# A two-layer attention kernel on one core: the first two query chunks walked side by side, group by group

## The chip, the core and the metric

The kernel runs on one core of a Trainium2 chip. TensorE (PE in the profile) multiplies, ScalarE (ACT) takes the exponentials, VectorE (DVE) copies and divides, SyncE (SP) issues most of the DMAs. The metric is device time in microseconds (us), the median over runs of the whole program.

## The reference, cut to what matters

Four blocks on one x of 2048 rows by 1024 columns, with 32 heads of 32 columns: A, B, A, B, each `x = x + block(layernorm(x))`. A is linear attention. B is softmax attention, and only B is touched by the change:

```python
def _B_ref(x, wqkv, wo):
    qkv = (x @ wqkv).reshape(B, S, 3, H, Dh).transpose(2, 0, 3, 1, 4)
    q, k, v = qkv[0], qkv[1], qkv[2]
    scores = einsum("bhqd,bhkd->bhqk", q, k) * (Dh ** -0.5)
    p = softmax(scores, axis=-1)
    o = einsum("bhqk,bhkd->bhqd", p, v)
    return o.transpose(0, 2, 1, 3).reshape(B, S, D) @ wo
```

## The kernel before

The program first records every operation with its engine, an estimated duration, its dependences, its buffers and a priority number. Then `Sched.run` plays the operations through once, engine by engine, lowest priority number first, nothing further than `WINDOW` = 40 ahead of the lowest number not yet begun, and no class of buffers over its `QUOTA`. The order that comes out is the order in which each engine's instructions are written. On the chip an engine does not leave that order.

There are two layers, each an A block and then a B block. The B block of a layer is `attention` (base number `at`). The 2048 queries are four chunks of 512 (`qc` 0 to 3), the 32 heads are eight groups of four (`g` 0 to 7). In this text a **unit** is one query chunk with one group. A unit has 64 score blocks (two head pairs `pp`, eight `d`, four `j`), each 128 keys by 512 queries. Three blocks make one **exp**: three score matmuls (line 827) into three PSUM banks, one ACT activation over 128x1536 (line 833), and then the matmuls of line 862, which multiply the exponentials by the values and by ones and add up in bank 6. The scores have banks 0 to 2 and 3 to 5 in turn, so PE can be at most two exps ahead of ACT. A unit has 21⅓ exps, a B block 32 units and 683 exps. At a unit's end DVE copies the accumulator (line 874), two DMAs move the sums (lines 881 and 883), DVE takes reciprocals (line 885) and multiplies (line 889); the result is an `oT` tile.

Everything else that PE does in the meantime goes through the one bank that is left, bank 7 (`FIL`). This text calls it **filler**: eight matmuls of 128x512 (line 586, in four **pieces** of two), and a DVE instruction that empties the bank. There are four kinds:

- `b_k(g, c, ...)`: keys of group g from chunk c of the input, 28 for groups 1 to 7; emptied by line 741, then four DMAs (line 733).
- `b_v(1, c, t, ...)`: values for groups 4 to 7, 16 of them.
- `b_q(g, qc, ...)`: queries of one unit, 31; emptied by line 749, then two DMAs (lines 751 and 752).
- `b_o` (layer 0) and `b_last` (layer 1, line 788): the output projection of a query chunk, once all eight of its `oT` tiles are there, 8 for a chunk. After chunk 3 they are not filler: they stand behind the attention, in any bank.

Before the change the units go chunk by chunk: (0,0), (0,1) ... (0,7), (1,0) ... (3,7). So all keys and values must be there by the end of the first eight units, and the numbers put `b_k` of group g at `at + 10*(g-1) + 1 + c`. Weights come as 256 KB loads (`w2`, line 446) or as 1 MB loads (`slab`).

Of the kernel before, what the change touches and what calls it, by code (L numbers as in the profile page):

```python
# [9 lines left out]
ACT = mybir.ActivationFunctionType  # L10
# [8 lines left out]
C512 = 512  # L19
# [26 lines left out]
class Sched:  # L46
# [87 lines left out]
    def run(self):  # L134
# [23 lines left out]
        while left:  # L158
# [56 lines left out]
WIDE = 3  # L215
WINDOW = 40.0
QUOTA = {"pk": 3, "pv": 2, "kv": 1, "ln": 2, "mm": 2, "cmp": 2, "bc": 2, "num": 1, "wt": 4, "fil": 2,
         "e": 6, "vp": 6, "E": 5, "q2": 3, "kt": 3, "w2": 8, "oT": 13, "T": 4, "den": 4, "lnt": 6, "lnw": 2,
         "eq": 8, "ns": 4, "cw": 6, "hl": 6, "oc": 2, "slab": 7, "fin": 4, "rs": 8}


# [8 lines left out]
MM = 0.2165  # L230
# [3 lines left out]
def kernel(  # L234
# [22 lines left out]
    B_w = B_wqkv.rearrange("(po pi) f -> pi po f", pi=P)  # L257
# [66 lines left out]
    op = sch.op  # L324
# [57 lines left out]
    xdone = [None] * NC  # L382
# [381 lines left out]
    def b_o(ft, c, prio, w, oT, banks):  # L764
        wb, ww, wd = w
        pb, pv = ps("fil", banks)
        m = mmg2(pb, pv, lambda po: ww()[:, po, :], lambda po: oT[po][1](),
                 [[oT[2 * i][2], oT[2 * i + 1][2]] for i in range(4)], wd,
                 [wb] + [oT[i][0] for i in range(G)], prio)
# [3 lines left out]
    def b_last(c, t, fc, prio, w, oT, banks, eng):  # L773

        wb, ww, wd = w
        pb, pv = ps("fil", banks)
        ts = slice(t * P, (t + 1) * P)
        xs = slice(c * C512 + t * P, c * C512 + (t + 1) * P)

        def resid():  # L780
            for k in range(4):
                nc.tensor.matmul(pv()[:, k * P:(k + 1) * P], lhsT=xT[:, 4 * fc + k, xs], rhs=ident[:],
                                 start=False, stop=(k == 3), skip_group_check=True)
        m = None
        for i in range(4):
# [4 lines left out]
            m = op("PE", 2 * MM, fn, flat([m, oT[2 * i][2], oT[2 * i + 1][2], wd[i]]),  # L790
                   [pb, wb, oT[2 * i][0], oT[2 * i + 1][0]], prio, mode="n")
        m = op("PE", 0.4, resid, [m], [pb], prio, mode="n")
        r_b, r_v = sb("fin", C512)
        e = evac(eng, r_v, pv, m, [pb, r_b], prio)
        dma(prio, lambda: nc.sync.dma_start(
            out=out[0, xs, fc * C512:(fc + 1) * C512], in_=r_v()), [e], [r_b], kb=128)

    def attention(base, kT, vT, q_of, gate):
# [10 lines left out]
        while i < len(units):  # L809
# [3 lines left out]
            s_b, s_v = ps("S", [tuple(range(lo, lo + w))])  # L813
            e_b, e_v = sb("E", WIDE * C512)
            qc, g, pp, d, j = grp[0]
            prio = base + 100 * qc + 10 * g + 5 * pp + 0.5 * d
            deps, bufs = [], []
            for u in grp:
                deps += flat([kT[u[1]][2][u[3] // 2], q_of[(u[0], u[1])][2]])
# [17 lines left out]
                e_of[u] = (e_b, e_v, x)  # L837
            i += w
            n += 1
        oTs = {}  # L840
        for qc in range(NC):
            oTs[qc] = {}
            for g in range(G):
                T = []
                for pp in range(2):
                    a_b, a_v = ps("acc", [(6,)])
                    last = None
                    for d in range(8):
                        prio = base + 100 * qc + 10 * g + 5 * pp + 0.5 * d
# [27 lines left out]
                prio = base + 100 * qc + 10 * g + 12  # L877
# [16 lines left out]
        return oTs  # L894


    xnA, xnB = {}, {}
    load_x()
    phi_ld = [dma(0.0, lambda j=j: nc.scalar.dma_start(
# [3 lines left out]
    for layer in range(2):  # L903
# [57 lines left out]
        for qc in range(NC):  # L961
            for g in range(G):
                if qc or g:
                    w = slab("w2", at + 100 * qc + 10 * g - 9, B_w[:, :, g * P:(g + 1) * P], P)
                    q_of[(qc, g)] = b_q(g, qc, at + 100 * qc + 10 * g - 6, w, FIL)
        oTs = attention(at, kT, vT, q_of, gate)
        last = layer == 1
        if last:
            bo_s = [slab("slab", at + 100 + fc, B_o[:, :, fc * C512:(fc + 1) * C512], C512) for fc in range(2)]
        for qc in range(NC):  # L970
            end = qc == NC - 1
            pr = at + 100 * (qc + 1)
            banks = ANY if end else FIL
            if last:
                for t in range(TB):
                    for fc in range(2):
                        b_last(qc, t, fc, pr + 20 + 8 * (2 * t + fc), bo_s[fc], oTs[qc], banks,
                               ("ACT", "DVE")[fc] if end else "DVE")
# [39 lines left out]
```

## Time and profile before

| | |
|---|---|
| median of 3 runs | 2840.84 us (2840.16 to 2841.62) |
| the profiled execution, its own time | 2833.51 us |
| its span, first to last instruction | 2831.7 us |
| PE, ACT, DVE busy over the span | 89%, 78%, 38% |
| first to last exp of layer 0 | 422.9 to 1406.3 us |
| first to last exp of layer 1 | 1815.1 to 2804.3 us |

The profiled execution is 7.3 us faster than the median; sums below are made against it. Busy shares are means over very unlike stages, and a busy PE need not be the bound: its matmuls are recorded with their latencies, and take longer when its clock is lower.

### The profile page before, as it was taken

The numbers are of one execution on the slowest core, as the hardware profiler recorded it, in microseconds if no ns is written. First come the engines' busy times: TensorE is split into PE (matmuls) and PEld (weight loads), VectorE is DVE, ScalarE is ACT, GpSimd is POOL, SyncE is SP. The second block draws the span as 40 slices with busy tenths as digits, with TensorE's granted clock in tenths as the row PEclk, the third lists the DMA queues.
The fourth block names the chain that finished last, engine by engine and source line by source line (L and its number), as shares of the span: only waits on it lengthen the run. The fifth ranks groups of instructions, "written<-read, shape, count | busy, mean of one in ns | idle before, by whom it ended". The sixth has DMA issues, their size and how long they took to land.

```text
span 2831.7 us, 42740 instructions
## 1 busy us (share of the span) xinstructions
PE 2520.0 (89%) x17984; PEld 804.2 (28%) x17984; DVE 1071.1 (38%) x1435; ACT 2211.7 (78%) x1931; POOL 22.4 (1%) x70
## 2 busy tenths in 40 slices
PE   6989989998898888888899999899988888888887
PEld 3543332222222222222144333222222222222222
DVE  4966652333222232222278666333322222222222
ACT  5325447789999999999842445477999999999996
POOL 0000000000000000000000000000000000000000
PEclk9999999999888888888699999899988978988987
DMA  8100003112201210210040000211211011011100
GB/s 179 53 31 3 5 9 75 36 35 47 45 19 29 46 26 21 47 33 14 22 123 8 31 5 2 54 38 32 68 40 27 25 27 29 23 27 36 25 16 23
DMA packets 213120, 101.40 MB, mean 36 GB/s; under 512 B 152512, under 2 KB 203712, under 8 KB 212928
## 3 DMA queue, kind: packets, MB, share of 16 engines
q1 hardware_dynamic: 208704, 94.42, 14.0%
q10 hardware_dynamic: 4224, 4.26, 0.6%
q8 instruction: 140, 2.29, 0.4%
q14 instruction: 52, 0.43, 0.1%
HBM read 50.40 MB, written 8.39 MB: 21 GB/s over the span
## 4 chain that ended last, share of the span: by engine, by line
PE 43%; ACT 39%; issue 10%; DVE 5%; DMA 2%; SPq 1%; ACTq 0%; DVEq 0%; POOL 0%; POOLq 0%
ACT arena L833 37%; PE psum L586 23%; PE psum L862 8%; PE psum L827 6%; SPq L389 1%; PE psum L788 1%; PE psum L677 1%; PE psum L562 1%; DVE arena L438 1%; DVE arena L434 1%; PE psum L368 1%; DMA arena<-arena 1%; ACT arena L404 1%; PE psum L664 1%; PE psum L701 0%
## 5 line engine op out<-in xcount | busy, mean ns | idle before, releaser
L833 ACT ACTIVATE arena<-psum 128x1536 bf16<-128x1536 f32 (+1 forms) x1366 | 1857.7, 1506 | 114.9 <-PE psum L827 86.7
L586 PE MATMUL psum<-arena 128*128 128x512 bf16 x3840 | 1029.3, 389 | 43.8 <-DVE arena L438 18.4
L862 PE MATMUL psum<-arena 128*32 128x512 bf16 x4096 | 856.7, 441 | 24.3 <-ACT arena L833 16.0
L862 PE MATMUL psum<-arena,ones_bf 128*32 128x512 bf16 x4096 | 856.9, 441 | 0.0
L827 PE MATMUL psum<-arena 32*128 32x512 bf16 x4096 | 600.8, 430 | 188.6 <-ACT arena L833 177.1
L586 PEld LDWEIGHTS <-arena 128*128 128x128 bf16 x3840 | 312.2, 98 | 510.2 <-issue 258.1
L827 PEld LDWEIGHTS <-arena 32*128 32x128 bf16 x4096 | 180.9, 92 | 712.4 <-issue 702.7
L862 PEld LDWEIGHTS <-arena 128*32 128x32 bf16 x4096 | 176.1, 96 | 514.2 <-issue 512.4
L874 DVE COPY arena<-psum 128x512 f32<-128x512 f32 x128 | 88.5, 691 | 555.1 <-PE psum L862 555.1
L885 DVE RECIPROCAL arena<-arena 128x128 f32<-128x128 f32 x256 | 217.7, 910 | 109.5 <-DMA arena<-arena 98.8
L749 DVE TENSOR_SCALAR arena<-psum 128x512 bf16<-128x512 f32 x64 | 44.2, 691 | 492.2 <-PE psum L827 353.8
L531 ACT ACTIVATE arena<-psum 128x512 bf16<-128x512 f32 x128 | 69.8, 603 | 163.9 <-PE psum L586 101.7
L862 PEld LDWEIGHTS <-ones_bf 128*32 128x32 bf16 x4096 | 177.9, 96 | 59.4 <-issue 57.5
L741 DVE CAST arena<-psum 128x512 bf16<-128x512 f32 x116 | 79.1, 682 | 273.8 <-PE psum L586 217.6
L404 ACT ACTIVATE arena<-xT 128x2048 bf16<-128x2048 bf16 x32 | 60.9, 1926 | 87.0 <-PE psum L586 47.2
L634 ACT ACTIVATE arena<-psum 128x512 bf16<-128x512 f32 x128 | 68.9, 600 | 60.5 <-PE psum L586 60.5
L434 DVE TENSOR_TENSOR arena<-xT,arena 128x1024 f32<-128x1024 bf16 x64 | 75.9, 1218 | 61.3 <-ACT arena L423 61.2
L740 ACT CAST arena<-psum 128x512 bf16<-128x512 f32 x44 | 25.5, 587 | 93.6 <-PE psum L586 72.1
L889 DVE TENSOR_TENSOR arena<-arena 64x512 bf16<-64x512 f32 x128 | 87.8, 686 | 7.1 <-PE psum L862 2.9
L788 PE MATMUL psum<-arena 128*128 128x512 bf16 x256 | 80.4, 413 | 5.7 <-DVE arena L889 5.5
L438 DVE TENSOR_TENSOR arena<-arena 128x1024 bf16<-128x1024 f32 x64 | 75.9, 1217 | 15.4 <-ACT arena L428 15.4
L543 DVE TENSOR_TENSOR arena<-psum,arena 128x1024 bf16<-128x1024 f32 x64 | 77.2, 1217 | 9.2 <-PE psum L586 8.1
(73 smaller groups left out, 901.2 us busy)
## 6 DMA issues: line engine op xcount, KB each, us to landing
arena<-in_B_wqkv_dram SPq DMA_DIRECT2D x80, 256.0 KB, 3.4
arena<-arena SPq DMA_DIRECT2D x128, 128.0 KB, 2.2
arena<-arena SPq DMA_DIRECT2D x256, 32.0 KB, 1.9
arena<-arena SPq DMA_DIRECT2D x128, 64.0 KB, 2.0
arena<-in_B_wo_dram SPq DMA_DIRECT2D x32, 256.0 KB, 3.6
arena<-in_A_wqkv_dram ACTq DMA_DIRECT2D x4, 1024.0 KB, 7.3
arena<-in_A_wo_dram SPq DMA_DIRECT2D x4, 1024.0 KB, 5.9
arena<-in_B_wqkv_dram SPq DMA_DIRECT2D x4, 1024.0 KB, 5.1
```

The costliest lines, as they stand in the source:

```text
L404: "ACT", act_us(2048), lambda hs=hs: nc.scalar.activation(out=xv()[:, hs, :], in_=xT[:, hs, csl(c)], func=ACT.Square),
L434: s1 = op("DVE", dve_us(1024), lambda pr=pr, w_v=w_v: nc.vector.tensor_tensor(out=w_v(), in0=xT[:, pr, csl(c)], in1=m_v().unsqueeze(1).to_ ...
L438: fin.append(op("DVE", dve_us(1024), lambda pr=pr, w_v=w_v: nc.vector.tensor_tensor(out=xv()[:, pr, :], in0=w_v(), in1=r_v().unsqueeze(1). ...
L586: nc.tensor.matmul(pv(), lhsT=lhs(po), rhs=rhs(po), start=(po == 0), stop=(po == PO - 1))
L741: return op("DVE", dve_us(512), lambda: nc.vector.tensor_copy(out=dst(), in_=src()), [dep], bufs, prio)
L788: nc.tensor.matmul(pv(), lhsT=oT[po][1]()[:, ts], rhs=ww()[:, po, :], start=(po == 0), stop=False, skip_group_check=True)
L827: nc.tensor.matmul(out=s_v()[:, x * C512:(x + 1) * C512], lhsT=kT[g][1]()[r, pp, d * P:(d + 1) * P], rhs=q_of[(qc, g)][1]()[r, (pp + j // ...
L833: ex = op("ACT", act_us(w * C512), lambda s_v=s_v, e_v=e_v, w=w: nc.scalar.activation(out=e_v()[:, 0:w * C512], in_=s_v(), func=ACT.Exp), ...
L862: nc.tensor.matmul(out=a_v()[col:col + 32, :], lhsT=v_v()[:, kc % 4, o:o + DH] if what == 0 else ones_bf[:], rhs=ev()[:, x * C512:(x + 1) ...
L874: cp = op("DVE", dve_us(512), lambda t_v=t_v, a_v=a_v: nc.vector.tensor_copy(out=t_v(), in_=a_v()), [last], [a_b, t_b], prio - 4)
L885: rc = [op("DVE", 128 * 8 / 960 + 0.12, lambda b=b, d_v=d_v, r_v=r_v: nc.vector.reciprocal(out=r_v()[:, b * P:(b + 1) * P], in_=d_v()[:, b ...
L889: s = [op("DVE", dve_us(512), lambda a=a, b=b, k=k, o_v=o_v, r_v=r_v, T=T: nc.vector.tensor_tensor(out=o_v()[a, :], in0=T[k][1]()[a, :], i ...
```

## The change

The units of chunks 0 and 1 now alternate: `turns` is (0,0), (1,0), (0,1), (1,1) ... (0,7), (1,7), then chunks 2 and 3 as before, and all numbers come from the place in `turns` (`pos`). Units are counted 0 to 31 in either order. A group's keys are now wanted only every second unit, and the numbers spread `b_k`, `b_v` and `b_q` accordingly. The output projections of chunks 0 and 1 come together, behind unit 15, and share their weight loads in layer 0 (8 fewer 256 KB loads). Those of chunk 3 get `TAIL` instead of `ANY` (all banks but 6), wait for the last score matmul (`after`) and have numbers 1 apart where they were 8 apart. The quota of `oT` tiles goes from 13 to 26.

```diff
-         ... "oT": 13, ...
+         ... "oT": 26, ...
+    TAIL = [(x,) for x in (7, 0, 1, 2, 3, 4, 5)]
...
+    turns = [(qc, g) for g in range(G) for qc in range(2)] + [(qc, g) for qc in range(2, NC) for g in range(G)]
+    pos = {t: i for i, t in enumerate(turns)}
...
-            for qc in range(NC) for g in range(G) for pp in range(2) for d in range(8) for j in range(4)
+            for qc, g in turns for pp in range(2) for d in range(8) for j in range(4)
...
-            prio = base + 100 * qc + 10 * g + 5 * pp + 0.5 * d
+            prio = base + 10 * pos[(qc, g)] + 5 * pp + 0.5 * d
...
-            w = slab("w2", at + 10 * (g - 1), B_w[:, :, D + g * P:D + (g + 1) * P], P)
+            pr = at + 10 * pos[(0, g)] - 19
+            w = slab("w2", pr - 1, B_w[:, :, D + g * P:D + (g + 1) * P], P)
-                b_k(g, c, at + 10 * (g - 1) + 1 + c, w, kT, FIL, "DVE")
+                b_k(g, c, pr + 4 * c, w, kT, FIL, "DVE")
...
-                b_v(1, c, t, at + 10 * c + 2.5 + 2 * t, bv_s[1], vT, FIL, "DVE")
+                b_v(1, c, t, at + 4.5 * (4 * c + t) + 2, bv_s[1], vT, FIL, "DVE")
...
-                    w = slab("w2", at + 100 * qc + 10 * g - 9, B_w[:, :, g * P:(g + 1) * P], P)
-                    q_of[(qc, g)] = b_q(g, qc, at + 100 * qc + 10 * g - 6, w, FIL)
+            pr = at + 10 * pos[(qc, g)] - 8
+            w = slab("w2", pr - 3, B_w[:, :, g * P:(g + 1) * P], P)
+            q_of[(qc, g)] = b_q(g, qc, pr, w, FIL)
...
-        for qc in range(NC):
-            end = qc == NC - 1
-            pr = at + 100 * (qc + 1)
-            banks = ANY if end else FIL
+        for qcs, p0, gap, banks in (((0, 1), 167, 9, FIL), ((2,), 247, 9, FIL), ((3,), 340, 1, TAIL)):
+            after = last_s if banks is TAIL else None
```

**How the order moves.** ACT's instructions stand in the same order before and after, all 1930. PE has the same 17984 matmuls; between the first and the last score of a B block they stand otherwise. Counted in the order, filler matmuls by unit:

| units | 0 to 4 | 5 to 7 | 0 to 7 | 8 to 15 | 16 to 23 | 24 to 30 |
|---|---|---|---|---|---|---|
| before, layer 0 | 336 | 96 | 432 | 128 | 128 | 104 |
| after, layer 0 | 212 | 128 | 340 | 162 | 184 | 106 |
| before, layer 1 | 336 | 96 | 432 | 160 | 160 | 136 |
| after, layer 1 | 212 | 128 | 340 | 180 | 230 | 138 |

The most in one unit is 72 before (units 1 to 3) and 48 after (unit 5). In layer 1 the counts hold four small matmuls of 128x128 for each `b_last`.

The first place is DVE in unit 1 of layer 0, from the copy of its first accumulator (line 874) to the last instruction ahead of unit 2's first copy. Lines 741 and 742 empty a filler bank of keys or values, 749 and 750 one of queries. Before:

```order
L874 COPY arena<-psum 128x512
L741 CAST arena<-psum 128x512 x3
L749 TENSOR_SCALAR arena<-psum 128x512
L741 CAST arena<-psum 128x512
L874 COPY arena<-psum 128x512
L741 CAST arena<-psum 128x512
L885 RECIPROCAL arena<-arena 128x128 x2
L741 CAST arena<-psum 128x512
L885 RECIPROCAL arena<-arena 128x128 x2
L889 TENSOR_TENSOR arena<-arena 64x512 x2
L741 CAST arena<-psum 128x512 x2
```

and now:

```order
L874 COPY arena<-psum 128x512
L742 CAST arena<-psum 128x512 x3
L874 COPY arena<-psum 128x512
L885 RECIPROCAL arena<-arena 128x128
L742 CAST arena<-psum 128x512
L885 RECIPROCAL arena<-arena 128x128 x3
L889 TENSOR_TENSOR arena<-arena 64x512 x2
L750 TENSOR_SCALAR arena<-psum 128x512
```

Nine filler banks were emptied in this stretch, now five.

The second place is SP where attention begins in layer 0: the last key DMAs of group 0 (line 733, now 734), and then the weight loads. The load of 128x8x512 is the 1 MB of weights for the values, 128x8x128 are 256 KB, the first of them for the keys of group 1. Before:

```order
L733 DMA arena<-arena 64x256 x12
L446 DMA arena<-in_B_wqkv_dram 128x8x512
L446 DMA arena<-in_B_wqkv_dram 128x8x128 x8
L733 DMA arena<-arena 64x256 x8
L881 DMA arena<-arena 64x512
```

and now:

```order
L734 DMA arena<-arena 64x256 x12
L447 DMA arena<-in_B_wqkv_dram 128x8x128
L447 DMA arena<-in_B_wqkv_dram 128x8x512
L447 DMA arena<-in_B_wqkv_dram 128x8x128 x6
L734 DMA arena<-arena 64x256 x4
```

The load for the first filler went from second to first place.

The third place is SP at the end of layer 0, up to the first weights of layer 1 (`wd_k`). `in_B_wo` are the weights of the output projection of chunk 3, lines 881 and 883 the sums of a unit. Before:

```order
L883 DMA arena<-arena 64x512
L446 DMA arena<-in_B_wo_dram 128x8x128
L881 DMA arena<-arena 64x512
L446 DMA arena<-in_B_wo_dram 128x8x128
L883 DMA arena<-arena 64x512
L446 DMA arena<-in_B_wo_dram 128x8x128 x6
L446 DMA arena<-wd_k 128x8x512
```

and now:

```order
L447 DMA arena<-in_B_wo_dram 128x8x128 x3
L881 DMA arena<-arena 64x512
L883 DMA arena<-arena 64x512
L881 DMA arena<-arena 64x512
L883 DMA arena<-arena 64x512
L447 DMA arena<-wd_k 128x8x512
```

Six of the eight loads stood behind the last unit's sums; now all stand ahead of the last two units' sums. On PE, after the last score matmul of each layer, eight matmuls of the output projection (four, two and two) now stand between the last groups of line 862; before, all of them stood behind.

## Rows read from the trace of the kernel before

**Rows 1.** The page: busy time, and PE, ACT, granted clock in 40 slices.

```profile
PE 2520.0 (89%) x17984; PEld 804.2 (28%) x17984; DVE 1071.1 (38%) x1435; ACT 2211.7 (78%) x1931; POOL 22.4 (1%) x70
...
PE   6989989998898888888899999899988888888887
...
ACT  5325447789999999999842445477999999999996
...
PEclk9999999999888888888699999899988978988987
```

**Rows 2.** Stretches of both layers: units 0 to 4, 5 to 7, 8 to 31.

```profile
422.94:610.83 187.89, 178.01 (x1296) 47.34 (x1293) 54.06 (x75) 146.67 (x109) 0.00 (x0) 0.98 0.23 50
610.83:696.79 85.96, 78.15 (x669) 22.38 (x669) 26.63 (x36) 85.96 (x66) 0.00 (x0) 1.00 0.17 41
696.79:1405.30 708.51, 618.44 (x4958) 160.13 (x4958) 177.19 (x237) 694.81 (x512) 0.00 (x0) 0.82 0.14 31
1815.08:2003.47 188.39, 179.56 (x1296) 47.56 (x1293) 54.05 (x75) 146.93 (x108) 0.00 (x0) 0.97 0.22 50
2003.47:2093.51 90.04, 83.27 (x669) 22.23 (x669) 26.63 (x36) 86.55 (x65) 0.00 (x0) 0.92 0.23 59
2093.51:2803.32 709.81, 610.79 (x5054) 168.06 (x5054) 176.15 (x237) 694.74 (x512) 0.00 (x0) 0.85 0.11 26
```

The columns are the stretch, its length, busy us (and instructions) of PE, PEld, DVE, ACT and POOL, the granted clock as a share, the DMA share, GB/s. An instruction that crosses an edge counts on both sides.

**Rows 3.** ACT at line 833, units 0 to 4, layer 0: releaser, idle us, times.

```profile
  PE psum L827: 35.4, 20
```

**Rows 4.** PE in time in unit 2, layer 0: start, length, instruction.

```profile
508.72 0.39 PE L827 MATMUL psum<-arena 32*128 32x512 bf16 x3
509.05 0.60 PE L586 MATMUL psum<-arena 128*128 128x512 bf16 x2
509.58 0.39 PE L862 MATMUL psum<-arena 128*32 128x512 bf16 x1
...
509.91 0.60 PE L586 MATMUL psum<-arena 128*128 128x512 bf16 x2
510.45 0.39 PE L827 MATMUL psum<-arena 32*128 32x512 bf16 x3
```

**Rows 5.** Stretches: units 1 to 4, then 5 and 6, layer 0.

```profile
462.62:610.83 148.21, 143.21 (x1048) 38.59 (x1047) 48.53 (x67) 116.54 (x87) 0.00 (x0) 1.00 0.14 33
610.83:668.36 57.53, 56.22 (x462) 15.45 (x461) 19.10 (x26) 57.53 (x44) 0.00 (x0) 1.00 0.18 44
```

**Rows 6.** The chain that ended last, at the first filler of layer 0.

```profile
422.93 5.84 DMA arena<-in_B_wqkv_dram
...
428.81 1.04 PE psum L586 x2
429.85 0.55 PE psum L862 x4
430.40 0.54 PE psum L827 x3
```

**Rows 7.** The same chain in unit 6 of layer 1.

```profile
2051.62 5.40 DMA arena<-arena
```

**Rows 8.** Stretch: units 30 and 31 of layer 0, without filler.

```profile
1344.80:1405.30 60.50, 54.44 (x390) 12.06 (x387) 12.29 (x16) 59.16 (x44) 0.00 (x0) 0.58 0.06 14
```

**Rows 9.** PE in time at the end of layer 0.

```profile
1406.70 2.55 PE L586 MATMUL psum<-arena 128*128 128x512 bf16 x11
1414.77 7.24 PE L586 MATMUL psum<-arena 128*128 128x512 bf16 x21 [5.52 <-DVE arena L889]
1422.35 7.14 PE L586 MATMUL psum<-arena 128*128 128x512 bf16 x32 [0.35 <-DVE xT L770]
```

**Rows 10.** PE in time at the end of layer 1.

```profile
2804.39 0.38 PE L862 MATMUL psum<-arena 128*32 128x512 bf16 x1 [0.30 <-ACT arena L833]
...
2815.76 3.27 PE L788 MATMUL psum<-arena 128*128 128x512 bf16 x14
...
2819.96 3.18 PE L788 MATMUL psum<-arena 128*128 128x512 bf16 x14
```

More of the change, by code (lines that the diff above doesn't have):

```diff
@@ L217 @@
 QUOTA = {"pk": 3, "pv": 2, "kv": 1, "ln": 2, "mm": 2, "cmp": 2, "bc": 2, "num": 1, "wt": 4, "fil": 2,
-         "e": 6, "vp": 6, "E": 5, "q2": 3, "kt": 3, "w2": 8, "oT": 13, "T": 4, "den": 4, "lnt": 6, "lnw": 2,
+         "e": 6, "vp": 6, "E": 5, "q2": 3, "kt": 3, "w2": 8, "oT": 26, "T": 4, "den": 4, "lnt": 6, "lnw": 2,
          "eq": 8, "ns": 4, "cw": 6, "hl": 6, "oc": 2, "slab": 7, "fin": 4, "rs": 8}
@@ L762, in b_v, with b_o @@
         done[t] = evac(eng, lambda: v_v()[:, t, :], pv, m, [pb, v_b], prio)
-    def b_o(ft, c, prio, w, oT, banks):
+    def b_o(ft, c, prio, w, oT, banks, after=None):
         wb, ww, wd = w
@@ L767, in b_o @@
         m = mmg2(pb, pv, lambda po: ww()[:, po, :], lambda po: oT[po][1](),
-                 [[oT[2 * i][2], oT[2 * i + 1][2]] for i in range(4)], wd,
+                 [[oT[2 * i][2], oT[2 * i + 1][2], after] for i in range(4)], wd,
                  [wb] + [oT[i][0] for i in range(G)], prio)
@@ L771, in b_o, with b_last @@
             out=xT[:, ft, csl(c)], in0=xT[:, ft, csl(c)], in1=pv(), op=ALU.add), [m], [pb], prio)
-    def b_last(c, t, fc, prio, w, oT, banks, eng):
+    def b_last(c, t, fc, prio, w, oT, banks, eng, after=None):
         wb, ww, wd = w
@@ L789, in fn @@
                                      start=(po == 0), stop=False, skip_group_check=True)
-            m = op("PE", 2 * MM, fn, flat([m, oT[2 * i][2], oT[2 * i + 1][2], wd[i]]),
+            m = op("PE", 2 * MM, fn, flat([m, oT[2 * i][2], oT[2 * i + 1][2], wd[i], after]),
                    [pb, wb, oT[2 * i][0], oT[2 * i + 1][0]], prio, mode="n")
@@ L839, in attention @@
             n += 1
-        oTs = {}
-        for qc in range(NC):
-            oTs[qc] = {}
-            for g in range(G):
+        oTs = {qc: {} for qc in range(NC)}
+        if True:
+            for qc, g in turns:
                 T = []
@@ L848, in attention @@
                     for d in range(8):
-                        prio = base + 100 * qc + 10 * g + 5 * pp + 0.5 * d
+                        prio = base + 10 * pos[(qc, g)] + 5 * pp + 0.5 * d
                         for u in range(2):
@@ L876, in attention @@
                     T.append((t_b, t_v, cp))
-                prio = base + 100 * qc + 10 * g + 12
+                prio = base + 10 * pos[(qc, g)] + 12
                 lo_, hi_ = slice(0, 64), slice(64, 128)
@@ L893, in attention @@
                 oTs[qc][g] = (o_b, o_v, s)
-        return oTs
+        return oTs, so
+    turns = [(qc, g) for g in range(G) for qc in range(2)] + [(qc, g) for qc in range(2, NC) for g in range(G)]
+    pos = {t: i for i, t in enumerate(turns)}
     xnA, xnB = {}, {}
@@ L961 @@
-        for qc in range(NC):
-            for g in range(G):
-                if qc or g:
-                    w = slab("w2", at + 100 * qc + 10 * g - 9, B_w[:, :, g * P:(g + 1) * P], P)
-                    q_of[(qc, g)] = b_q(g, qc, at + 100 * qc + 10 * g - 6, w, FIL)
-        oTs = attention(at, kT, vT, q_of, gate)
+                b_v(1, c, t, at + 4.5 * (4 * c + t) + 2, bv_s[1], vT, FIL, "DVE")
+        for qc, g in turns[1:]:
+            pr = at + 10 * pos[(qc, g)] - 8
+            w = slab("w2", pr - 3, B_w[:, :, g * P:(g + 1) * P], P)
+            q_of[(qc, g)] = b_q(g, qc, pr, w, FIL)
@@ L967 @@
+        oTs, last_s = attention(at, kT, vT, q_of, gate)
         last = layer == 1
         if last:
-            bo_s = [slab("slab", at + 100 + fc, B_o[:, :, fc * C512:(fc + 1) * C512], C512) for fc in range(2)]
-        for qc in range(NC):
-            end = qc == NC - 1
-            pr = at + 100 * (qc + 1)
-            banks = ANY if end else FIL
-            if last:
[L975 to L978, printed above, removed]
+            bo_s = [slab("slab", at + 160 + fc, B_o[:, :, fc * C512:(fc + 1) * C512], C512) for fc in range(2)]
@@ new lines @@
+        for qcs, p0, gap, banks in (((0, 1), 167, 9, FIL), ((2,), 247, 9, FIL), ((3,), 340, 1, TAIL)):
+            after = last_s if banks is TAIL else None
+            if last:
+                for qc in qcs:
+                    for t in range(TB):
+                        for fc in range(2):
+                            i = 2 * (TB * (qc - qcs[0]) + t) + fc
+                            b_last(qc, t, fc, at + p0 + gap * i / len(qcs), bo_s[fc], oTs[qc], banks,
+                                   ("ACT", "DVE")[fc] if banks is TAIL else "DVE", after)
@@ L979 @@
             else:
-                adds = []
+                adds = {qc: [] for qc in qcs}
                 for ft in range(G):
-                    w = slab("w2", pr + 10 + 8 * ft, B_o[:, :, ft * P:(ft + 1) * P], P)
-                    adds.append(b_o(ft, qc, pr + 20 + 8 * ft, w, oTs[qc], banks))
-                xdone[qc] = adds
+                    w = slab("w2", at + p0 + gap * ft - 8, B_o[:, :, ft * P:(ft + 1) * P], P)
+                    for qc in qcs:
+                        adds[qc].append(b_o(ft, qc, at + p0 + gap * ft, w, oTs[qc], banks, after))
@@ L986 @@
+                for qc in qcs:
+                    xdone[qc] = adds[qc]
     for o in sch.run():
```

## The prediction, made before the changed kernel ran

> **What bounds the kernel now.** The page comes first. Its slices [rows 1] show PE at eight or nine tenths nearly everywhere, and ACT at nine only from the middle of each B block on; at the start of both B blocks ACT stands at seven. So there are two regimes, and the view by stretches [rows 2] cuts them apart. In units 5 to 7 of layer 0 ACT is busy for 85.96 of 85.96 us: ACT is the bound, at 85.96 / 64 = 1.343 us for an exp. Units 8 to 31 take 708.5 and 709.8 us for 511 exps from start to start, 1.387 and 1.389: nearly the same bound, with small waits. Units 0 to 4 take 187.9 and 188.4 us for 106⅔ exps, 1.76 each; ACT is idle for some 41 us there, PE for 10. What ACT waited for [rows 3] was the score matmuls of line 827, 35.4 us in 20 waits. So in units 0 to 4 PE is the bound, and what it does beyond attention is filler.
>
> What PE pays is read from its instructions in time [rows 4], at full clock, from start to start: 0.33 us for the three score matmuls of an exp (508.72 to 509.05), 0.33 for one group of line 862 (509.58 to 509.91), of which an exp has one and a half, and 0.54 for a piece of filler (509.91 to 510.45). So an exp costs PE 0.33 + 1.5 x 0.33 = 0.83, and a piece 0.54. Units 1 to 4 bear this out [rows 5]: 280 filler matmuls are 140 pieces, 75.6 us; the other 72.6 us over 85⅓ exps are 0.85. I take 0.84. Units 5 and 6 come to 42⅔ x 0.84 + 41 x 0.54 = 57.9, measured 57.5: there PE and ACT are both full.
>
> **The change, step by step.** *Units 0 to 7.* The same keys and values now have sixteen units instead of eight; filler in units 0 to 7 falls from 432 matmuls to 340, and no unit has over 48. By unit, with 17.9 us of PE for attention, 0.27 for each filler matmul and ACT's 28.6 as the floor: 28.7, 29.8, 29.3, 30.3, 28.7, 30.9, 28.6, 29.3, together 235.6 us. (ACT alone would need 170⅔ x 1.343 = 229.2.) So PE and ACT end up level. DVE's emptying of bank 7, five instead of nine in a unit, lies beside this.
>
> *The first filler.* By the same prices units 0 to 4 should have taken 106⅔ x 0.84 + 168 x 0.54 = 180.3; they took 7.6 and 8.1 more. The chain shows where most of it went [rows 6]: the first filler waited for weights that landed 5.84 us after 422.93, behind the 1 MB load, and the work after the wait ran at the half clock. Now the 256 KB load goes first. Nothing before shows it alone, so the loss lies between 0 and 7.6; I take 3, below the middle, as the wait's cause is gone. That makes 238.6 us against 273.9 (187.89 + 85.96) in layer 0 and 278.4 in layer 1: 35.3 + 39.8 = 75.1 us gained.
>
> *Units 8 to 31* get the filler that left, 92 and 92 matmuls more. Their pace hardly hangs on filler: 1.387 over all of them, and 60.5 / 43 = 1.407 in the last two without any filler, at a granted clock of 0.58 [rows 8]. I take no change. The bounds are 1.343 (22 us less in a layer) and 1.407 (10 more).
>
> *The end of layer 0.* In the rows [rows 9] the first 21 output matmuls after 1414.77 took 7.24 us, the next 32 took 7.14; at the latter's 0.22 the 21 are 4.7, so 2.5 went on weights that stood on SP behind the last sums. They now stand ahead: 2.5 less, between 0 and 2.5 if SP is late anyway. Against it: eight output matmuls, 2.2 us, now stand between the last score and the last line 862, and the last unit's copy, DMAs, reciprocals and multiplies queue behind that. PE idles there for 0.30 us at a time [rows 10], so not all of it is hidden: 1.2 more, bounds 0 and 2.2, in each layer.
>
> *The end of layer 1.* Two output tiles took 4.2 us of PE (2815.76 to 2819.96) [rows 10], with 14 matmuls, 4 small ones, 2, 4. Now 16 matmuls and then 8 small ones stand in a row, two tiles end together, and the next pair waits for a bank to be emptied: I take 0.5 for each of three pairs, 1.5 more, bounds 0 and 3.
>
> Nothing is priced for the eight loads saved, or for `oT`'s larger quota: nothing waits for either in these rows.
>
> The sum: -75.1 - 2.5 + 2 x 1.2 + 1.5 = -73.7. The profiled execution, 2833.5, would become 2759.8; the median stands 7.3 above it, so I forecast **2767 us**.
>
> **The rivals.** *The clock takes the gain back (slower).* In units 0 to 4 PE is never without work. Spread out, PE's work could leave gaps, the granted clock could fall from the 0.98 and 0.97 of these stretches to the 0.82 of units 8 to 31 [rows 2], and matmuls at the half level (1.2 instead of 2.4 GHz) take 0.54, 0.55 and 1.04 instead of 0.33, 0.33 and 0.54 [rows 6]. With a share h of the time at the half level PE does 1 - 0.42h of its work, since half-clock work runs at about 0.58 of the speed. At 0.82 (h = 0.36) 235.6 us become 278, with 3 for the start 281: 7 and 2 us slower than now, 2767 + 75 + 9 = 2851 us. It decides below a granted clock of about 0.84. For it speaks that PE in the last two units, at 90% busy, had 0.58 [rows 8]. Against it speak units 5 and 6 [rows 5]: 41 pieces on 42⅔ exps, as thin as units 0 to 7 will be (170 on 170⅔), and a clock of 1.00 with PE busy for 56.2 of 57.5 us. A PE that falls behind has no gaps, so this would mend itself. Chance 0.07. The Trainium skill (TensorE: Matmul & The Clock Gate, "What's actually happening") says that the throttled state is the default and activity lifts it, which speaks against any thinning of PE's work; by that rule alone the time would lean to this rival, and units 5 and 6 show that this load is still enough.
>
> *New waits at unit starts.* Every unit now needs another chunk's queries, and every second one another group's keys. The order leaves at least eight exps, 11 us, between the last filler matmul for queries and the unit that wants them. (Before it was less than one exp in units 1 to 4.) A DMA of keys behind larger transfers has taken 5.40 us [rows 7]. If each of the 15 further unit starts in both layers cost 2 us, 60 us would be lost: 2827. Likelier is that some do, and that PE and ACT, both full, trip over each other: at 1.45 instead of 1.38 for an exp, 12 us a layer, 2791. Chance of something in this band 0.14.
>
> *Units 8 to 31 gain too.* The filler moved there is up to 46 pieces, and units 5 to 7 had their 1.343 with more filler and a full clock. At 1.36 each layer gains another 14 us: 2739. Against it: units with more and with less filler run at like pace. Chance 0.14.
>
> *The change doesn't do what it says.* The planner could have kept the filler early. The order excludes that, 340 against 432; what would remain is that PE's filler was not the cause of the waits, and the time would stay within 0.2%. [Rows 3] name the score matmuls as what came late, so 0.03.
>
> **How the numbers follow.** The forecast has 0.62, for itself within 2752 to 2785: the start's 0 to 7.6 in each layer, the ends' few us, and 1% of pace in units 8 to 31. A range for 8 in 10 leaves out the clock, the upper part of the new waits and the far end of the gain in units 8 to 31: 2738 to 2806. Faster by over 0.2% (5.7 us, about what a measurement of this kernel can tell from no change): 0.62 + 0.14 + 0.14 = 0.90; within it 0.03; slower 0.07.
>
> **What would show it.** In the profile after, units 0 to 7 should take about 239 us in each layer, at 1.38 to 1.40 an exp, with ACT busy for over 95% of that and the granted clock at 0.95 or more; the first wait for `in_B_wqkv` should be gone from the chain. Units 8 to 31 should take 709 us again, and the last exp of each layer come some 35 to 40 us sooner after the first. From the last exp of layer 0 (1406.3) to the end of the output matmuls (1422.35 + 7.14) [rows 9] the 23.2 us should become about 22. Wrong would be: ACT's idle time in units 0 to 7 ended by score matmuls while PE is idle too (a wait for keys or queries), or a clock under 0.9 there.

## The result

The changed kernel takes 2759.04 us (median of 4 runs, 2758.15 to 2763.5) against 2840.5 us (median of 4, 2836.79 to 2841.62): the ratio is 0.9719, with a 95% interval of 0.9702 to 0.9735. The forecast was 2767 us. The profiled execution took 2758.15 us, with a span of 2756.4 us against 2831.7.

The page of the changed kernel answers to [rows 1]; its last line is the group of the exps, with their idle time and what ended most of it. (253 matmuls lack records in this trace, so PE's busy time is a little more than it shows.)

```profile
PE 2448.6 (89%) x17731; PEld 799.7 (29%) x17984; DVE 1071.8 (39%) x1435; ACT 2205.3 (80%) x1931; POOL 22.4 (1%) x70
...
PE   5989988999888888989889899899998888889887
...
ACT  5325548999999999999843354499999999999995
...
PEclk9999999999987998787699999999999889988987
...
L834 ACT ACTIVATE arena<-psum 128x1536 bf16<-128x1536 f32 (+1 forms) x1366 | 1851.5, 1536 | 41.2 <-PE psum L828 30.7
```

The same group before the change:

```profile
L833 ACT ACTIVATE arena<-psum 128x1536 bf16<-128x1536 f32 (+1 forms) x1366 | 1857.7, 1506 | 114.9 <-PE psum L827 86.7
```

The sevens of ACT at the start of both B blocks are gone. Before the change ACT was idle ahead of the exps for 114.9 us, 86.7 of it ended by score matmuls; now 41.2 and 30.7. ACT's own work is the same within 0.4% (1857.7 and 1851.5 us).

The stretches of the changed kernel, cut as in [rows 2] (columns as there): units 0 to 4, 5 to 7, 8 to 31 of layer 0, then of layer 1.

```profile
422.23:573.35 151.12, 142.55 (x1142) 39.29 (x1161) 43.29 (x59) 144.61 (x109) 0.00 (x0) 0.98 0.23 53
573.35:662.56 89.21, 85.53 (x697) 24.10 (x708) 29.40 (x40) 86.31 (x65) 0.00 (x0) 1.00 0.16 38
...
662.56:1370.04 707.48, 619.17 (x4997) 165.46 (x5049) 185.53 (x249) 694.49 (x513) 0.00 (x0) 0.84 0.14 32
1780.66:1931.86 151.20, 142.42 (x1142) 39.27 (x1161) 43.30 (x59) 144.49 (x109) 0.00 (x0) 0.98 0.23 53
1931.86:2020.99 89.13, 85.54 (x697) 24.09 (x708) 29.40 (x40) 86.35 (x65) 0.00 (x0) 1.00 0.16 38
...
2020.99:2723.50 702.51, 607.11 (x5090) 171.66 (x5144) 184.45 (x249) 693.22 (x512) 0.00 (x0) 0.88 0.12 31
```

Units 0 to 4 fell from 187.9 and 188.4 us to 151.1 and 151.2; units 5 to 7 went from 86.0 and 90.0 to 89.2 and 89.1. The difference of the two spans is laid out from starts of exps:

| stretch | before | after | difference | predicted |
|---|---|---|---|---|
| to the first exp | 422.9 | 422.2 | -0.7 | 0 |
| units 0 to 7, layer 0 | 273.9 | 240.3 | -33.5 | -35.3 |
| units 8 to 31, layer 0 | 708.5 | 707.5 | -1.0 | 0 |
| last exp of layer 0 to first of layer 1 | 409.8 | 410.6 | +0.8 | -1.3 |
| units 0 to 7, layer 1 | 278.4 | 240.3 | -38.1 | -39.8 |
| units 8 to 31, layer 1 | 709.8 | 702.5 | -7.3 | 0 |
| last exp of layer 1 to the end | 28.4 | 32.9 | +4.5 | +2.7 |
| sum | | | -75.3 | -73.7 |

### The profile page after: what moved, and what is told of

Read it like the earlier page. It is cut to its first block, busy times and chain, and to the rows that moved or that the text cites. A ratio compares the mean times of both kernels' runs of the same rounds, so it can differ in the third digit from the quotient of the medians.

```text
span 2756.4 us, 42381 instructions
## 1 busy us (share of the span) xinstructions
PE 2448.6 (89%) x17731; PEld 799.7 (29%) x17984; DVE 1071.8 (39%) x1435; ACT 2205.3 (80%) x1931; POOL 22.4 (1%) x70
## 4 chain that ended last, share of the span: by engine, by line
PE 43%; ACT 39%; issue 10%; DVE 5%; DMA 2%; SPq 0%; ACTq 0%; DVEq 0%; POOL 0%; POOLq 0%
ACT arena L834 36%; PE psum L587 22%; PE psum L862 9%; PE psum L828 6%; PE psum L789 1%; PE psum L563 1%; PE psum L678 1%; DVE arena L439 1%; PE psum L369 1%; ACT arena L405 1%; DVE arena L435 1%; DMA arena<-in_A_wqkv_dram 1%; DMA arena<-arena 1%; PE psum L665 1%; PE psum L702 0%
## 5 line engine op out<-in xcount | busy, mean ns | idle before, releaser
L834 ACT ACTIVATE arena<-psum 128x1536 bf16<-128x1536 f32 (+1 forms) x1366 | 1851.5, 1536 | 41.2 <-PE psum L828 30.7
L587 PE MATMUL psum<-arena 128*128 128x512 bf16 x3630 | 985.2, 387 | 57.8 <-DVE arena L439 18.3
L828 PE MATMUL psum<-arena 32*128 32x512 bf16 x4096 | 590.8, 423 | 162.2 <-ACT arena L834 149.8
L862 PEld LDWEIGHTS <-arena 128*32 128x32 bf16 x4096 | 181.8, 95 | 531.6 <-issue 529.3
L536 DVE TENSOR_REDUCE arena<-arena 128x32 f32<-128x1024 bf16 x64 | 76.1, 1211 | 11.5 <-ACT arena L532 10.1
```

Source lines behind the costliest of these rows:

```text
L587: nc.tensor.matmul(pv(), lhsT=lhs(po), rhs=rhs(po), start=(po == 0), stop=(po == PO - 1))
L828: nc.tensor.matmul(out=s_v()[:, x * C512:(x + 1) * C512], lhsT=kT[g][1]()[r, pp, d * P:(d + 1) * P], rhs=q_of[(qc, g)][1]()[r, (pp + j // ...
L834: ex = op("ACT", act_us(w * C512), lambda s_v=s_v, e_v=e_v, w=w: nc.scalar.activation(out=e_v()[:, 0:w * C512], in_=s_v(), func=ACT.Exp), ...
L862: nc.tensor.matmul(out=a_v()[col:col + 32, :], lhsT=v_v()[:, kc % 4, o:o + DH] if what == 0 else ones_bf[:], rhs=ev()[:, x * C512:(x + 1) ...
```

## The experiments

The theory is that of the prediction: before, PE was the bound in units 0 to 4, through filler; spread over sixteen units the filler leaves PE and ACT level. Two rivals to it in units 0 to 4: late weights and queries at unit starts, not filler, held ACT up; or the alternation itself gives the gain. Then come edits that try the prediction's smaller terms. Each ratio is to the kernel before, run beside it on the same chip.

**1. Before, the queries of chunk 0 one unit earlier.** In `before`:

```diff
-                    w = slab("w2", at + 100 * qc + 10 * g - 9, ...)
-                    q_of[(qc, g)] = b_q(g, qc, at + 100 * qc + 10 * g - 6, w, FIL)
+                    lead = 10 if qc == 0 else 0
+                    w = slab("w2", at + 100 * qc + 10 * g - 9 - lead, ...)
+                    q_of[(qc, g)] = b_q(g, qc, at + 100 * qc + 10 * g - 6 - lead, w, FIL)
```

> The kernel before, chunk by chunk, with one number changed: the queries of chunk 0 are made 10 earlier, so that their last filler matmul stands 17 exps or more ahead of their unit instead of less than one. Filler in units 0 to 7 is the same 432 matmuls. Theory (PE's filler is what makes units 0 to 4 slow): units 0 to 7 keep their 274 us in each layer, the time stays at 2840 within 6. Rival (the queries came at the last moment and their DMAs were what was waited for, and the change won by its longer leads): most of the 35 us of ACT's idle time at units 0 to 4 goes in each layer, 2775 to 2800.

Measured: 2827.76 us, ratio 0.9949 (0.9931 to 0.9968). That is 11.6 us below the kernel before beside it (2839.38), where the theory allowed 6, and far above the rival's 2775 to 2800. Its stretches, units 0 to 7 of both layers:

```profile
424.13:693.08 268.95, 260.52 (x1964) 67.77 (x1962) 80.94 (x111) 234.55 (x173) 0.00 (x0) 0.97 0.21 48
...
1819.74:2087.30 267.56, 259.19 (x1964) 67.70 (x1962) 80.85 (x111) 234.57 (x172) 0.00 (x0) 0.97 0.23 55
```

So 5 and 11 us went, of the 34 and 38 that the change gains. Where they went is seen when unit 0 is taken by itself. Unit 0 and units 1 to 7 of layer 0, before and then in this run:

```profile
422.94:462.62 39.68, 34.79 (x251) 8.75 (x249) 5.53 (x8) 30.13 (x24) 0.00 (x0) 0.91 0.55 113
462.62:696.79 234.17, 221.37 (x1716) 60.97 (x1716) 75.16 (x103) 202.50 (x151) 0.00 (x0) 1.00 0.15 36
```

```profile
424.13:458.07 33.94, 32.37 (x237) 8.08 (x234) 5.51 (x8) 30.29 (x23) 0.00 (x0) 0.95 0.64 129
458.07:693.08 235.01, 228.15 (x1731) 59.68 (x1728) 75.44 (x104) 204.25 (x150) 0.00 (x0) 0.97 0.15 36
```

Unit 0 gained 5.7 us, and 7.3 in layer 1 (41.27 to 33.93), of which four filler matmuls fewer are 1.1 by their price. The queries of unit 0 are not moved by the edit; but the weights for the queries of unit 1 are now loaded ahead of the 1 MB, they feed the first filler, and PE no longer waits for a load there as it does in [rows 6]. In units 1 to 7, where late queries would be felt, nothing was gained in layer 0 and 3.5 us in layer 1 (237.16 to 233.63). So of the first rival the late weights were worth up to 5.7 and 7.3 us, and the late queries nothing in one layer and at most 3.5 in the other. The rest is filler. Counted in this trace by unit it is 52, 62, 70, 56, 80, 56, 44 and 12 matmuls; by the prediction's prices (17.9 us for attention, 0.27 for a filler matmul, 28.6 as the floor) that gives 267 us, where 269.0 and 267.6 were measured.

**2 and 3. Thin values, in the kernel before and in the changed one.** The values of groups 4 to 7 are made of two matmuls instead of eight, which leaves out three quarters of their sum.

```diff
+        if fc == 1:
+            def one():
+                for po in range(2):
+                    nc.tensor.matmul(pv(), lhsT=xv()[:, po, ts], rhs=ww()[:, po, :], start=(po == 0), stop=(po == 1))
+            m = op("PE", 2 * MM, one, flat([fin, wd]), [pb, xb, wb], prio, mode="n")
+        else:
+            m = mmg2(pb, pv, ...)
```

In the kernel before:

> The kernel before with the values of groups 4 to 7 made from a quarter of their sum (2 matmuls of 8), which leaves out part of the computation: 48 pieces less in units 0 to 4 of each layer. Queries come as late as before. Theory (PE-bound there at 0.84 us an exp and 0.54 a piece): units 0 to 7 go from 274 to 249 us, 25 less in each layer, 2790. Rival (waits for late queries): units 0 to 4 stay near 1.7 us an exp, 2825 or more.

In the changed kernel:

> The changed kernel with the same quarter of the values' sum, 48 pieces less in units 0 to 7 of each layer. Theory (after the change PE and ACT are level there, so ACT takes over at once): units 0 to 7 go from 240 to about 235 us, ACT's 229 and the start, 2748. Rival (PE's filler is still what bounds): 26 less in each layer, 2707. Second rival (what is left over 229 is waits for DMAs and evictions): no change, 2759.

Measured: 2779.56 us, ratio 0.9788 (0.9768 to 0.9809), and 2754.67 us, ratio 0.9702 (0.968 to 0.9723). Units 0 to 7 of the kernel before, thinned:

```profile
423.23:669.99 246.76, 234.31 (x1868) 63.12 (x1866) 80.79 (x111) 232.17 (x172) 0.00 (x0) 0.97 0.23 52
...
1791.11:2040.48 249.37, 236.95 (x1868) 63.53 (x1866) 80.67 (x111) 232.87 (x172) 0.00 (x0) 0.96 0.25 59
```

and of the changed kernel, thinned:

```profile
422.39:661.17 238.78, 216.59 (x1796) 60.48 (x1793) 74.24 (x102) 230.84 (x172) 0.00 (x0) 0.97 0.21 49
...
1777.71:2014.90 237.19, 216.16 (x1796) 60.23 (x1793) 74.15 (x102) 230.50 (x172) 0.00 (x0) 0.97 0.22 49
```

The same cut takes 27 and 29 us from these units before the change, and 1.5 and 3 after. Before, PE's filler was the bound; after, taking PE's work away gains next to nothing, because ACT is there with 230.8 and 230.5 us. What is left over ACT's own time are waits, not filler.

**4. The changed kernel with the old numbers for keys and values.**

```diff
-            pr = at + 10 * pos[(0, g)] - 19
+            pr = at + 10 * (g - 1) + 1
...
-                b_k(g, c, pr + 4 * c, w, kT, FIL, "DVE")
+                b_k(g, c, pr + c, w, kT, FIL, "DVE")
...
-                b_v(1, c, t, at + 4.5 * (4 * c + t) + 2, ...)
+                b_v(1, c, t, at + 10 * c + 2.5 + 2 * t, ...)
```

> The changed kernel, units alternating, but keys and values with the numbers of the kernel before, so that they are made as early as there: filler by unit 1.31, 1.31, 1.50, 1.69, 1.73, 1.17, 1.03, 0.38 pieces an exp instead of about 1.0 throughout. Theory (the gain is the spreading): units 0 to 7 take 272 us instead of 240 in each layer, 2825. Rival (the gain is the alternation by itself, keys used for two units in turn and longer leads): below 2775.

Measured: 2820.3 us, ratio 0.9925 (0.9899 to 0.9952). Units 0 to 7:

```profile
422.86:692.98 270.12, 259.35 (x1965) 68.25 (x1963) 80.54 (x111) 234.10 (x173) 0.00 (x0) 0.97 0.20 49
...
1814.61:2085.54 270.93, 259.31 (x1965) 68.22 (x1963) 80.54 (x111) 234.01 (x172) 0.00 (x0) 0.97 0.20 48
```

With units alternating, but the filler early, they take nearly what the first experiment's take (269.0 and 267.6), and 3.7 and 7.5 us less than before the change. So in these units the alternation by itself gives at most a small part of the 34 and 38 us; it is what allows the spreading.

**5. The changed kernel, keys' weights loaded earlier.**

```diff
-            w = slab("w2", pr - 1, B_w[:, :, D + g * P:D + (g + 1) * P], P)
+            w = slab("w2", pr - 10, B_w[:, :, D + g * P:D + (g + 1) * P], P)
```

> The changed kernel with the weight loads of the keys 9 numbers earlier, so that the two 256 KB loads (keys of group 1, queries of unit 1) both stand ahead of the 1 MB load on SP; before, the keys' load stood third, behind it. Theory (what unit 0 still loses, 34.5 us against 28.7 by PE's prices, is the first filler's wait for those weights, and the half clock after it): unit 0 takes about 29.5 us in both layers, 10 us less in all, 2749. Rival (the loss is the start of the units itself: an empty pipeline and a clock that fell before): unit 0 stays at 34, 2759.

The reason for it stands in the chain of the changed kernel, where the first filler of layer 0 stands as it did in [rows 6]:

```profile
421.54 6.47 DMA arena<-in_B_wqkv_dram
428.05 1.03 PE psum L587 x2
```

Measured: 2750.92 us, ratio 0.9685 (0.9668 to 0.9701). Unit 0 of layer 0 in the changed kernel, then (second fence) with the earlier weights:

```profile
422.23:456.77 34.54, 29.47 (x225) 7.69 (x226) 4.15 (x6) 29.94 (x23) 0.00 (x0) 0.90 0.49 104
```

```profile
420.93:453.78 32.85, 30.71 (x233) 8.15 (x230) 4.06 (x6) 29.76 (x24) 0.00 (x0) 0.95 0.53 109
```

The load is gone from the chain, and units 0 to 7 take 238.5 and 238.9 us. Unit 0 took neither the theory's 29.5 nor the rival's 34: it still takes 3.3 us more than 22 starts at ACT's 1.343 (29.5). ACT's waits of that unit, and PE ahead of the longest of them, show why:

```profile
426.90 1.45 ACT L834 ACTIVATE arena<-psum 128x1536 bf16<-128x1536 f32 x1 [0.48 <-PE psum L862]
...
439.12 16.23 ACT L834 ACTIVATE arena<-psum 128x1536 bf16<-128x1536 f32 x12 [2.16 <-PE psum L828]
```

```profile
424.66 1.03 PE L587 MATMUL psum<-arena 128*128 128x512 bf16 x2
...
434.50 0.39 PE L828 MATMUL psum<-arena 32*128 32x512 bf16 x3
...
438.62 0.60 PE L828 MATMUL psum<-arena 32*128 32x512 bf16 x6
```

Two short waits of ACT, 0.48 and 0.45 us, come behind pieces at the half level (424.66). The long one, 2.16, comes at full clock: between 434.50 and 438.62 PE's order has four pieces and five groups of line 862 in a row ahead of the next scores. So the load was worth 1.7 us in unit 0 and 1.9 in layer 1, and most of what is left there is the order of PE's instructions. That the time came within 2 us of the theory's 2749 is luck: units 0 to 7 gave 3.3 us of the 8.6 that the profiled execution gained, and the others (2.5 of them between the layers) were not traced.

**6. The changed kernel, with all seven banks for the last projections.** `TAIL` names seven banks, but the class `fil` has a quota of two buffers, so only two of them were ever in use.

```diff
-         ... "fin": 4, ...
+         ... "fin": 8, ...
...
-        pb, pv = ps("fil", banks)
+        pb, pv = ps("tail" if after else "fil", banks)
...
-        return oTs, so
+        return oTs, last
```

`fin` are the output buffers, eight instead of four. The middle lines are those of `b_o` and `b_last`. The last line makes these projections wait for the last matmul of line 862 instead of the last score.

> The changed kernel with the output projection of chunk 3 waiting for the last matmul of line 862 instead of the last score, in a class of buffers of its own (no quota, so all seven banks of TAIL are used instead of two) and eight output buffers instead of four. Theory: the end of each layer is PE work that two banks hold back; six of eight matmuls of seven tiles fit into the wait for the last sums. Last line 862 2.1 and 2.8 us sooner after the last exp, then 7 us less in layer 0 (22 matmuls left instead of 52) and 9 less in layer 1: 2738. Rival (the end is set by emptying the banks and by the stores): only the 4.9 us of the sooner last matmul, 2754.

Measured: 2741.16 us, ratio 0.9648 (0.9632 to 0.9664). PE in time at the end of layer 1, first the changed kernel:

```profile
2723.91 1.49 PE L789 MATMUL psum<-arena 128*128 128x512 bf16 x3 [0.33 <-issue]
...
2735.83 1.46 PE L789 MATMUL psum<-arena 128*128 128x512 bf16 x3 [6.88 <-DVE arena L889]
...
2738.39 4.27 PE L789 MATMUL psum<-arena 128*128 128x512 bf16 x15 [0.25 <-ACT arena L741]
...
2743.60 3.61 PE L789 MATMUL psum<-arena 128*128 128x512 bf16 x16 [0.49 <-ACT arena L741]
...
2748.16 3.61 PE L789 MATMUL psum<-arena 128*128 128x512 bf16 x16 [0.49 <-ACT arena L741]
```

and then with seven banks:

```profile
2721.80 9.66 PE L789 MATMUL psum<-arena 128*128 128x512 bf16 x44
2731.30 0.61 PE L783 MATMUL psum<-ident,xT 128*128 128x128 bf16 x8
2731.74 1.03 PE L789 MATMUL psum<-arena 128*128 128x512 bf16 x4
```

With two banks the tiles go in pairs, and between pairs PE waits for a bank to be emptied. With seven, PE does most of the work that needs only the first six `oT` tiles while the last unit's sums are on their way, instead of being idle for 6.88 us; what then is left of two tiles are four matmuls and eight small ones. From the last exp to the end 32.9 us become 21.3; between the layers 410.6 become 402.5. The edits were not run apart, but the traces part them: the last group of line 862 begins 2.8 and 2.1 us sooner after the last exp (1.1 us behind it in both layers), which is the later start of the projections; the other 8.8 and 6.0 us are the banks with the output buffers, and these two are not told apart.

**7. The changed kernel with useless pieces in the thin units.** 142 and 108 pieces that compute nothing of use go into bank 7, in units 10 to 31 of layer 0 and 1, up to 15 a unit, to hold the granted clock up. (The expectation counts 150 in layer 0; the numbers of `WARM` add up to 142.)

```diff
+        for u, n in WARM[layer].items():
+            for k in range(n):
+                e = -(-64 * u // 3) + 21 * k // n
+                pb, pv = ps("warm", FIL)
+                ...
+                        nc.tensor.matmul(pv(), lhsT=ident[:], rhs=..., start=(x == 0), stop=(x == 1))
+                op("PE", 2 * MM, warm, [sos[e]], [pb], at + 10 * u + 10 * k / n, mode="n")
```

> The changed kernel with extra pieces of two matmuls into bank 7, on constants and read by nobody, in units 10 to 31 wherever filler is thin, up to about 0.7 pieces an exp: 150 pieces in layer 0, 108 in layer 1. The output is the same. Theory (units 8 to 31 lose their 0.05 us an exp over ACT's 1.34 because the granted clock falls, mean 0.84 and 0.88, where filler is under 0.4 pieces an exp; 0.64 and more had 1.00): more work makes the stretch shorter, clock 0.95 or more, 1.36 an exp, 12 us less in each layer, 2735. Rival (the small waits have another cause, and the added work only gets in the way): 2759 or more.

Measured: 2760.97 us, ratio 0.9719 (0.9703 to 0.9735): the time of the changed kernel. Units 8 to 29 and 30 to 31 of layer 0, in the changed kernel:

```profile
662.56:1311.23 648.67, 568.50 (x4622) 153.47 (x4674) 173.24 (x233) 636.89 (x471) 0.00 (x0) 0.86 0.14 32
1311.23:1370.04 58.81, 50.67 (x381) 11.99 (x375) 12.29 (x16) 57.59 (x44) 0.00 (x0) 0.65 0.17 32
```

and with the useless pieces:

```profile
663.74:1316.71 652.97, 597.06 (x4905) 165.06 (x4903) 172.94 (x233) 633.20 (x470) 0.00 (x0) 0.95 0.14 32
1316.71:1373.01 56.30, 49.94 (x431) 14.94 (x429) 12.28 (x16) 56.30 (x43) 0.00 (x0) 1.00 0.18 33
```

The clock rose, and where the pieces lie evenly (units 30 and 31) the pace went to 1.34. The others lost 4.3 us. The expectation's reading of the granted clock by filler does not hold unit by unit either: unit 24 of layer 1 in the changed kernel, with 28 filler matmuls, had 0.80. The longest wait of ACT there, in PE's and ACT's instructions in time (line 829 are the scores, 836 the exps, 980 the useless pieces; line 862's, here 864, left out):

```profile
1147.96 0.61 PE L829 MATMUL psum<-arena 32*128 32x512 bf16 x3
...
1149.05 1.03 PE L980 MATMUL psum<-phi,ident 128*128 128x512 bf16 x2
...
1150.57 1.03 PE L980 MATMUL psum<-phi,ident 128*128 128x512 bf16 x2
...
1153.49 0.39 PE L829 MATMUL psum<-arena 32*128 32x512 bf16 x3
...
1153.99 1.45 ACT L836 ACTIVATE arena<-psum 128x1536 bf16<-128x1536 f32 x1 [3.89 <-PE psum L829]
```

Four pieces and four groups of line 862 stand in a row ahead of the next scores, two of the pieces at the half level, and ACT sits idle for 3.89 us. In layer 0's units 8 to 31 ACT waited 17.2 us for scores in 13 waits, against 9.0 in 15; in layer 1's 13.4 in 14, against 7.0 in 14, the longest 3.4 against 0.8.

**8. Experiments 5, 6 and 7 together.**

> The three edits together: keys' weights first, seven banks and the later start of the last projection, extra pieces where filler is thin. They touch different stretches, so by the theories their gains add: 10 + 21 + 24, 2704. By the rivals of all three 2754.

Measured: 2737.77 us, ratio 0.9636 (0.962 to 0.9651): 34 us over the 2704 that the theories add up to and 16 below the 2754 of the rivals. How much of the gain is that of the two edits that gained alone is seen without the third, in the next run.

**9 and 10. Experiments 5 and 6 together, without useless pieces, and with them in units 30 and 31 alone** (`WARM = {0: {30: 15, 31: 12}, 1: {30: 15, 31: 12}}`).

> The changed kernel with two edits together: the keys' weights of a group are loaded ten numbers ahead, and the output groups behind the last exponential use seven banks. Alone they gave 2750.92 and 2741.16 us against 2759.04, that is -8.1 and -17.9. Theory (the two act in different places, the start of a layer and its end, so they add): 2759.0 - 26.0 = 2733.0 us, units 0 to 7 at 238.6 us in each layer, the end of layer 1 at 21.3 us, 402 us between the layers. Rival (a part of the gain of the early keys' weights lay at the end of the layers and is the same gain as that of the banks; with the useless pieces beside them the two gave 2737.8): 2736 to 2738 us. Leaving out the useless pieces is then worth nothing to 4 us.

> As the kernel with the two edits, and with 15 and 12 useless pieces spread over units 30 and 31 alone of each layer (these two units went from 1.41 and 1.39 us an exponential to 1.35 and 1.33 in layer 0 when all thin units had such pieces, while other units lost as much as those gained). Theory (the half level of the clock costs something only where it meets a queue of scores that is late, as at the end of a layer; pieces in these two units alone keep the gain and none of the loss): 2 units x 21.3 x 0.06 = 2.6 us in each layer at most, so 5 us less than the kernel with the two edits, 2728 us, with units 30 and 31 at 57.5 us instead of 60. Rival (each useless piece is 0.43 us of the tensor engine and these units gain nothing net): the same time within 1.5 us.

Measured: 2730.63 us, ratio 0.9617 (0.9602 to 0.9633), the fastest of all, 28.4 us below the changed kernel where 26.0 were expected: the gains add. Experiment 8, which has the useless pieces besides, took 7.1 us more, though the two intervals touch; so these gave nothing there, and by the medians they cost time. With pieces in units 30 and 31 alone 2732.54 us, 0.9622 (0.9607 to 0.9636), the same within the intervals. Units 30 and 31 without pieces took 57.38 and 58.07 us; with them, in layer 0 and then in layer 1:

```profile
1310.23:1366.29 56.06, 49.74 (x432) 14.96 (x432) 12.28 (x16) 56.06 (x44) 0.00 (x0) 1.00 0.12 24
...
2651.72:2710.16 58.44, 52.32 (x437) 14.92 (x434) 12.29 (x16) 56.45 (x44) 0.00 (x0) 0.95 0.04 10
```

1.3 us gained in one layer, 0.4 lost in the other. The theory of the clock is given up as a source of time.

## Why the prediction was right, and where its steps were off

**Units 0 to 7: right in mechanism and size.** 240.3 us in each layer against 238.6, ACT busy for 96% of it, the granted clock 0.98 and 1.00. Experiments 1 to 4 show that it was the filler and its spreading. The prices of PE's instructions carry it: units 1 to 7 took 205.8 us, where the prediction's list gives 206.9 (235.6 less 28.7 for unit 0).

**The first filler: this step failed.** The prediction took 3 us for what is left of the start "as the wait's cause is gone", and expected the load gone from the chain. It is still there, with 6.47 us, and unit 0 took 34.5 us where the prediction's list has 28.7: 5.8 more, not 3 (5.0 over ACT's pace, 29.5). Units 1 to 7 happened to give 1.1 of that back. The load that the order shows first is 256 KB, but it carries the weights for the queries of unit 1; the 1 MB load comes second and the keys' weights, which the first filler wants, third. "The load for the first filler went from second to first place", ahead of the prediction, is therefore wrong: the row names the tensor, not the columns. Experiment 5 mends it and gets 1.7 us in unit 0; most of the rest is the row of four pieces ahead of scores that its trace shows. How much the wait cost before, experiment 1 shows: up to 5.7 and 7.3 us, most of the 7.6 and 8.1 by which units 0 to 4 exceeded their prices.

**Units 8 to 31: 0 predicted, -1.0 and -7.3 measured.** They take the moved filler at no cost. Of the 7.3 us in layer 1, 6.6 lie in units 16 to 23, where 230 filler matmuls stand instead of 160. These units before, in the changed kernel, and in experiment 4, which has the same 230 there:

```profile
2328.01:2567.77 239.76, 208.88 (x1699) 56.36 (x1699) 59.48 (x80) 233.02 (x173) 0.00 (x0) 0.84 0.11 27
```

```profile
2255.99:2489.20 233.21, 203.06 (x1747) 59.97 (x1769) 62.40 (x85) 231.40 (x172) 0.00 (x0) 0.92 0.12 31
```

```profile
2321.60:2554.27 232.67, 205.89 (x1769) 60.12 (x1769) 62.56 (x86) 231.18 (x172) 0.00 (x0) 0.93 0.13 32
```

ACT waited there for scores 8 times before, 4.6 us in all, and 3 times after, 1.3 us. More filler, a higher granted clock and less time together are what the third rival said of these units, and here it came about, in a third of the units of one layer. Which of them makes it is open: in units 16 to 23 of layer 0, 184 filler matmuls instead of 128 went with 0.87 instead of 0.84 and gained 2.0 us (238.0 to 236.0), and experiment 7, which raised the clock over units 10 to 31, gained nothing in sum.

**The end of layer 0: -1.3 predicted, +0.8 measured.** The weights that stand earlier on SP save 1.9 of the 2.5 us: from the first output matmul behind the last multiply to the last one it took 14.7 us before (1414.77 to 1429.49) and 12.8 now. But in the changed kernel the last line 862 ends 3.5 us after the last exp's start, and the eight matmuls of the output projection in its way are these:

```profile
1370.44 1.10 PE L587 MATMUL psum<-arena 128*128 128x512 bf16 x3 [0.34 <-issue]
...
1371.80 0.60 PE L587 MATMUL psum<-arena 128*128 128x512 bf16 x2
...
1372.67 0.60 PE L587 MATMUL psum<-arena 128*128 128x512 bf16 x2
...
1381.65 12.83 PE L587 MATMUL psum<-arena 128*128 128x512 bf16 x50 [6.86 <-DVE arena L889]
```

(Of the first four and of the last group a few lack records.) The first ran at the half level. The last group of line 862 begins 3.2 us after the last exp's start, and 3.9 in layer 1 (2727.37, after 2723.50), where before it was 1.1 (2804.39 [rows 10], after 2803.32 [rows 2]). So they cost 2.1 and 2.8 us, where the prediction took 1.2, below its own 2.2 for full clock. From the last score on there is no exp ahead that hides them, so the full price was the right one, and more. From the end of the last exp to the end of the output matmuls it is 23.4 us, where 23.2 should have become about 22.

**The end of layer 1: +2.7 predicted, +4.5 measured.** 2.8 instead of 1.2 for the eight matmuls, as above, which leaves 1.7 where 1.5 was taken for the pairs. "The next pair waits for a bank" is what the rows show, 0.25, 0.49 and 0.49 us.

**The median.** The sum was made for the profiled execution: -73.7 predicted, -75.4 measured (2833.51 to 2758.15). That these lie so near is in part luck: the single lines of the table miss by up to 7.3 us, in both directions. Most of the 8 us between the forecast and the median are the 7.3 us by which the profiled run of before stood below its median; that of after stands only 0.9 below.

**The rivals.** The clock stayed at 0.98 and 1.00 in the units that were thinned: units 5 and 6 of before were the right witness. New waits at unit starts cost little: the thinned kernel of experiment 3 keeps 7.9 and 6.7 us over ACT's busy time in units 0 to 7, and 6.8 and 4.7 of that lie in unit 0 (36.74 and 34.62 us, with ACT busy for 29.98 and 29.93).

## What to carry to other kernels

Price PE's work unit by unit against the pace of the engine that should be the bound: where the sum of the prices exceeds it, the work to move is the one with a later due time, and the gain is the excess. Before trusting that a transfer is first in line, see which consumer's part it carries, not only its tensor's name. And a list of banks does nothing beyond the quota of its class: at the end of a block count the banks that the trace shows in use.

## What was not expected of the hardware

A higher granted clock was no time gained. In units 8 to 31 it rose from 0.84 and 0.88 to 0.95 and 0.96, and they took 709.3 and 703.9 us instead of 707.5 and 702.5; ACT waited longer for scores, 17.2 us against 9.0 and 13.4 against 7.0. The longest wait has the useless pieces in front of the scores; the others were not followed one by one. The Trainium skill (TensorE: Matmul & The Clock Gate, "What's actually happening") says that activity releases the throttle of the clock; these rows agree with that. They also show how little a lower clock costs in a stretch where ACT is the bound: in units 30 and 31, 58.81 us at 0.65 against 56.30 at 1.00 in experiment 7, and in layer 1 of experiment 10 0.4 us the other way.

A load of 256 KB that lands 3.3 us after its issue in the median of its kind took 6.47 us as the third of a row of loads on one queue, behind one of 1 MB.
